# First batch of an FFT filter and softplus MLP on one core: stage A in pairs, stage B from SBUF, later weight conversions

## The chip, the cores and the metric

The kernel runs on one core of a Trainium2 chip. The metric is the device time of one execution in microseconds (us); lower is better. Before the change three runs took 2556.89, 2555.26 and 2554.69 us, with a median of 2555.26 us.

The core has five engines that run side by side, each through its own queue in order: PE (matrix products; its weight loads are listed as PEld), DVE (the vector engine), ACT (the scalar engine), POOL (GpSimd) and SP, which here only issues DMAs. ACT and POOL issue DMAs too. All DMAs run on 16 DMA engines.

## The reference

```python
X = np.fft.rfft(x, axis=1)                      # x: 8 x 3072 x 256
Y = X * (filt_r + 1j * filt_i)[None, :, :]
y = np.fft.irfft(Y, n=3072, axis=1).reshape(8 * 3072, 256)
h = y @ w_in                                    # 256 x 2048
g = np.maximum(h, 0.0) + np.log1p(np.exp(-np.abs(h)))
out = (g @ w_out).astype(np.float32)            # 2048 x 256
```

[...]

## The kernel before

**Arithmetic.** Every float32 product is three passes over operands split as hi + lo (`split_mm`, L64). A split is a rounding copy (hi) and a subtraction (lo): `hi_lo`, L75.

**Transform of one batch.** Stage A: sums and differences of the sequence's halves (`a_sum`), split, and multiplied by a 128-point matrix `ca`, for 12 values of n2 (`a_mm`, results `psa`). Between A and B the data has to change partition and free axes. Stage B: 13 groups u of 120 rows (the last has 96), split (`inh`, `inl`), multiplied by `cb`, then by the filter `fr`, `fi` on DVE (three operations t, L181 to L185, and one sum on POOL, L186). The product is split again (`zh`, `zl`) and multiplied by `cc` in stage C (`psc`, copied to `co`). After a second change of axes, stage D (`di`, `psd`, `sd`, `y`) gives 512 tokens of MLP input (`yT`) for each of 6 blocks.

**Change of axes.** In batches 1 to 7 both go through DRAM (`s1`, `s2`). In batch 0, A's results stay in SBUF (`first_s1`, 128 partitions); `b_load` (L144) copies group u by two DMAs (one for each half h) from 10 neighbouring partitions of `first_s1` to 120 partitions of a tile `bi`, and loads `fr` (256 KB) and `fi` (128 KB) of that group. These four DMAs for each u are issued by SP; `bi` and the filter's tile `ft` have three buffers each. `co` goes to DRAM (`s2`) by a DMA on ACT's queue and comes back by `d_load`.

**MLP.** 48 blocks of 512 tokens, 8 steps each: `mm1` (12 products into `h`), three ACT operations, `soft` (three DVE operations of 128x1024: `s` L294, `gh` L296, `gl` L298), and two steps later `mm2` (12 products into `o`). Pieces of the next batch's transform stand between them in fixed slots. I call the DVE operation L294 of step i "s(i)", counted from the MLP's first step.

**Weights.** Sixteen blocks k of 512 columns (0 to 7 for w_in, 8 to 15 for w_out) are loaded as raw 64-bit words and converted: six DVE operations (`weight`, L344 to L357), one ACT copy and two POOL operations (`weight_ends`, L371 to L373). `LOADS`, `CONVERSIONS` and `WEIGHTS` say when: block 0 after A's tenth piece, 1 and 2 at A's end, 3 after the first piece of B, 8, 9 and 4 after C, 5 and 11 between D and the MLP, then one block in each of the steps 0 to 6 (10, 6, 7, 12, 13, 14, 15). Within a step the conversion's operations stand between and behind the three of `soft`.

**Order.** Everything is emitted in one hand-made order (`manual_schedule`): for batch 0 by `first`, which walks through the list `seq` of pieces and loads and prepares ahead; afterwards by `Run` with its slots. Tile pools add the waits for buffers. Buffers of raw weights are shared with other tiles (`TAGS`).

Of the kernel before, what the change touches and what calls it, by code (L numbers as in the profile page):

```python
# [12 lines left out]
bits, and hi hi + hi lo + lo hi is summed in float32.  # L13
"""
# [27 lines left out]
TAGS = {1: "in", 2: "ca", 4: "in", 5: "in", 8: "in", 11: "ca"}  # whose buffers they use, if not the output's  # L42
# Twice the upper word of the least normal float32, as float64.
# [4 lines left out]
def fft_mlp(ctx: ExitStack, tc: tile.TileContext, x, fr, fi, ca, cb, cc, cd, w_in, w_out, out):  # L48
# [14 lines left out]

    def split_mm(ps, lhs, rhs, first=True, last=True):  # L64
# [18 lines left out]
    class Batch:  # L83
# [5 lines left out]
        def engines(self, first):  # L89
            """Where hi and lo of loaded data are worked out: nothing else waits for them in the first transform."""  # L90
            return (nc.vector, nc.gpsimd) if self.b or first else (nc.scalar, nc.vector)

        def a_load(self, i):
            if i == 0 and self.b:
                self.s1 = dram.tile([2, P, N2, D], F32, tag="s1", name="s1")
            if self.b or i < 6:
                xt = work.tile([P, 2, 512], F32, tag="in", name="x", bufs=3)
            else:
                xt = start.tile([P, 2, 512], F32, name=f"x{i}")
# [18 lines left out]
        def a_prep(self, i):  # L118
            if self.b or i == 0:
                self.a_sum(i)  # L120
            st = self.t.pop(("as", i))
            if self.b == 0 and i + 1 < N2:
                self.a_sum(i + 1)
            self.t["ap", i] = hi_lo(st, P, "in", *self.engines(0))

        def a_mm(self, i):
# [7 lines left out]
            if self.b == 0:  # L134
# [494 lines left out]
```

## Time and profile before

| | us |
|---|---|
| median of three runs | 2555.26 |
| span of the profiled execution, first to last instruction | 2552.2 |
| start of the first A piece on PE | 8.17 |
| start of the first B piece on PE | 36.68 |
| s(0), the first softplus operation on DVE | 137.71 |
| s(7) | 198.34 |

The profile gives no time of its own beside its span; the median of the runs is 3.1 us above the span, for what lies around it. Times in the tables of the profile are counted from the span's start. In answers that list instructions, the columns are start, duration, engine, line of the kernel, operation, output and inputs, and, in brackets, how long the engine had been idle and what released it. In the view of busy time by stages, the columns are the stage, its length, busy time and number of instructions on PE, PEld, DVE, ACT and POOL, the granted PE clock (1 is full), the mean busy share of the 16 DMA engines, and GB/s.

### The profile page before, as it was taken

How to read it: one execution, taken by the hardware profiler on the slowest of the kernel's cores; microseconds unless marked ns; L12 is line 12 of the kernel's file. 1: busy time of each engine (PE TensorE's matmuls, PEld its weight loads, DVE VectorE, ACT ScalarE, POOL GpSimd, SP SyncE). 2: the span in 40 equal slices, each digit the busy share in tenths (PEclk: the TensorE clock that was granted, in tenths of full speed). 3: DMA queues.
4: the chain of work that ended last, by engine and by line, in shares of the span. 5: the costliest groups of instructions: out<-in, count | busy, mean ns of one | idle time of the engine just before them, and what ended most of it. 6: DMA issues, size and time to landing. Idle time of an engine off the chain costs nothing.

```text
span 2552.2 us, 31099 instructions
## 1 busy us (share of the span) xinstructions
PE 2459.7 (96%) x11232; PEld 2026.3 (79%) x11232; DVE 2050.1 (80%) x2575; ACT 1494.7 (59%) x1742; POOL 747.3 (29%) x610
## 2 busy tenths in 40 slices
PE   4579999999999999999999999999999999999999
PEld 3258778888888888888888888888888888888887
DVE  7799896888878897789878888688887898766665
ACT  3355556656656665666566566566665666665555
POOL 4444341333213332233313333143221433111110
PEclk7589999999999999999999999999999999999999
DMA  7724432433224431343223432243422533111100
GB/s 209 200 83 142 124 106 73 133 117 98 71 85 143 119 98 52 104 147 107 80 76 121 130 85 82 90 128 97 117 70 70 170 103 91 44 42 34 42 17 17
DMA packets 144244, 249.97 MB, mean 98 GB/s; under 512 B 12772, under 2 KB 62052, under 8 KB 144092
## 3 DMA queue, kind: packets, MB, share of 16 engines
q1 hardware_dynamic: 91740, 149.98, 19.5%
q0 software_dynamic: 14112, 50.83, 6.9%
q10 hardware_dynamic: 38240, 47.20, 5.9%
q8 instruction: 88, 1.44, 0.2%
q14 instruction: 64, 0.52, 0.1%
HBM read 172.46 MB, written 72.35 MB: 96 GB/s over the span
## 4 chain that ended last, share of the span: by engine, by line
PE 88%; DVE 6%; DMA 2%; issue 2%; ACT 1%; SPq 0%; POOL 0%; ACTq 0%; DVEq 0%; POOLq 0%
PE h L67 39%; PE o L67 39%; PE psd L241 3%; PE psa L67 2%; PE psb L67 2%; PE psc L67 2%; DMA bi<-s 1%; DVE s L294 1%; DMA x<-in_x 1%; DVE gh L296 0%; DVE gl L298 0%; DVE raw L349 0%; DVE inh L73 0%; DVE raw L353 0%; DVE p L345 0%
## 5 line engine op out<-in xcount | busy, mean ns | idle before, releaser
L67 PE MATMUL h<-yT,wi 128*128 128x512 f32 x4608 | 1120.6, 392 | 12.7 <-DVE s L294 11.2
L67 PEld LDWEIGHTS h<-yT,wi 128*128 128x128 f32 x4608 | 859.7, 189 | 192.2 <-DVE s L294 10.2
L67 PE MATMUL o<-gh,wo 128*128 128x512 f32 x3072 | 953.1, 391 | 5.5 <-ACT ob L321 4.7
L285 ACT ACTIVATE s<-h 128x1024 f32<-128x1024 f32 x384 | 394.8, 1028 | 722.5 <-PE h L67 684.4
L67 PEld LDWEIGHTS o<-gh,wo 128*128 128x128 f32 x3072 | 568.8, 189 | 121.2 <-ACT ob L321 5.1
L294 DVE SCALAR_TENSOR_TENSOR s<-h,s 128x1024 f32<-128x1024 f32 x384 | 468.0, 1219 | 180.2 <-ACT s L287 177.9
L67 PE MATMUL o<-gl,wo 128*128 128x512 f32 x1536 | 600.3, 391 | 2.8 <-DVE gl L298 2.8
L298 DVE TENSOR_TENSOR gl<-s,gh 128x1024 fp32r<-128x1024 f32 x384 | 471.5, 1228 | 36.5 <-DVE gh L296 1.8
L286 ACT ACTIVATE s<-s 128x1024 f32<-128x1024 f32 x384 | 407.8, 1062 | 12.2
L287 ACT ACTIVATE s<-s 128x1024 f32<-128x1024 f32 x384 | 407.6, 1062 | 12.2
L296 DVE CAST gh<-s 128x1024 fp32r<-128x1024 f32 x384 | 313.2, 816 | 36.5 <-DVE s L294 2.3
L67 PEld LDWEIGHTS o<-gl,wo 128*128 128x128 f32 x1536 | 288.9, 188 | 65.8 <-DVE gl L298 4.1
L267 POOL TENSOR_TENSOR yT<-y,yT 128x512 fp32r<-128x512 f32 x94 | 126.2, 1343 | 607.1 <-DVE yT L73 607.1
L186 POOL TENSOR_TENSOR t<-t,t 128x512 f32<-128x512 f32 x104 | 147.7, 1420 | 405.7 <-DVE t L185 404.2
L79 POOL TENSOR_TENSOR inl<-bi,inh 120x512 fp32r<-120x512 f32 (+1 forms) x100 | 132.6, 1326 | 289.0 <-issue 114.3
L79 POOL TENSOR_TENSOR dil<-di,dih 128x512 fp32r<-128x512 f32 x94 | 121.4, 1291 | 208.5 <-DVE dih L73 140.4
L253 DVE TENSOR_TENSOR sd<-psd,ev 128x256 f32<-128x256 f32 x192 | 80.6, 420 | 114.9 <-ACT ev L252 114.7
L79 POOL TENSOR_TENSOR inl<-st,inh 128x512 fp32r<-128x512 f32 x84 | 118.1, 1406 | 166.8 <-DVE inh L73 165.6
L79 DVE TENSOR_TENSOR zl<-t,zh 128x512 fp32r<-128x512 f32 x104 | 90.5, 870 | 56.6 <-ACT zh L71 54.4
L241 PE MATMUL psd<-cd,dih 128*128 128x256 f32 x384 | 100.9, 285 | 11.5 <-ACT dih L71 9.8
L241 PE MATMUL psd<-cd,dil 128*128 128x256 f32 x384 | 101.8, 286 | 3.0 <-DVE dil L79 3.0
L67 PE MATMUL psb<-inh,cb_sb 120*128 120x512 f32 (+1 forms) x224 | 74.1, 416 | 20.1 <-ACT inh L71 19.1
(60 smaller groups left out, 1808.1 us busy)
## 6 DMA issues: line engine op xcount, KB each, us to landing
ft<-in_fr SPq DMA_DIRECT2D x104, 256.0 KB
x<-in_x SPq DMA_DIRECT2D x48, 512.0 KB
ca<-in_ca POOLq DMA_DIRECT2D x48, 512.0 KB, 4.7
cd<-in_cd POOLq DMA_DIRECT2D x48, 512.0 KB, 4.1
di<-s SPq DMA_DIRECT2D x96, 256.0 KB
out<-ob SPq DMA_DIRECT2D x48, 512.0 KB
s<-co ACTq DMA_DIRECT2D x96, 240.0 KB
s<-ao ACTq DMA_DIRECT2D x84, 256.0 KB
```

The costliest lines, as they stand in the source:

```text
L67: nc.tensor.matmul(out=ps, lhsT=lhs[a], rhs=rhs[b], start=first and k == 0, stop=last and k == 2)
L79: lo_eng.tensor_sub(out=lo[:p], in0=src, in1=hi[:p].bitcast(F32))
L186: nc.gpsimd.tensor_add(out=t1, in0=t1, in1=t2)
L241: nc.tensor.matmul(out=ps[:, h].rearrange("p k n -> p (k n)"), lhsT=ds[k][:, h, 128 * c:128 * c + 128], rhs=cdt[:, h, j].rearrange("p k n ...
L253: nc.vector.tensor_add(out=s[:, j], in0=ps[:, :, 0], in1=ev)
L267: lo_eng.tensor_sub(out=lo[:, c], in0=y, in1=hi[:, c].bitcast(F32))
L285: nc.scalar.activation(out=a, in_=h, func=AF.Abs)
L286: nc.scalar.activation(out=a, in_=a, func=AF.Exp, scale=-1.0)
L287: nc.scalar.activation(out=a, in_=a, func=AF.Ln, bias=1.0)
L294: nc.vector.scalar_tensor_tensor(out=a, in0=h, scalar=0.0, in1=a, op0=ALU.max, op1=ALU.add)
L296: nc.vector.tensor_copy(out=hi, in_=a)
L298: nc.vector.tensor_sub(out=lo, in0=a, in1=hi.bitcast(F32))
```

## The change

It concerns the first batch and the order of the weights; the only edit to later batches is that `b_load` now issues two DMAs instead of one.

- **Stage A by pairs** (`first_a`): two values of n2 are handled as one, with 1024 columns for hi, lo, the PSUM tile and its copy `ao`. There are again 12 sums and differences of 512 columns. x has three buffers instead of six tiles; the loads of the pairs 3, 4 and 5 are issued as buffers come free, and those of 4 and 5 behind the copies of the pairs 0 and 1 on SP.
- **A straight to B's tile**: `ao` goes by four DMAs for each pair (two of 120 rows, two of 8) into `s1_b`, an SBUF tile that has stage B's layout for all 13 groups. The constant matrix's columns are put in another order, so that a DMA of 120 rows writes 10 partitions that lie 12 apart. `bi` and its 26 DMAs are gone.
- **Filter ahead** (`filter_load`): each of the 13 groups has its own tile. Groups 0 to 5 are loaded between the copies of the last three pairs, 6 to 12 behind the raw blocks 0, 1, 2.
- **lo in B**: on DVE for u = 0, 1, 2, 3, 5, 7, 9, 11 (before 0, 2, 3, 7), otherwise on POOL.
- **First block's inverse on chip** (`c_mm`): beside the DMA to DRAM, two small DMAs on SP bring each `co` of batch 0 into block 0's tile `di`.
- **Weights**: no block is converted in A. Block 0 is converted ahead of B's first preparation, 1 at B's end, 2 and 8 between C and D, and the other twelve in the steps 0 to 7: (3, 9), (4), (5, 10), (6, 11), (7, 12), (13), (14), (15).
- The late pools lie on the other side of SBUF and wait tile by tile.

```diff
-LOADS = {("a", 8): (0,), ("a", 10): (2, 3), ("c", 9): (9,), ("c", 11): (8, 4), ("d", 1): (11,), ("y", 0): (5,)}
-CONVERSIONS = {("a", 9): (0,), ("a", 11): (1, 2), ("b", 0): (3,), ("c", 12): (8, 9, 4)}
-WEIGHTS = (5, 11), (10,), (6,), (7,), (12,), (13,), (14,), (15,)
+WEIGHTS = (3, 9), (4,), (5, 10), (6, 11), (7, 12), (13,), (14,), (15,)
...
         def b_load(self, u):
-            if self.b == 0:
-                for h in range(2):
-                    nc.sync.dma_start(
-                        out=bt[:p, 256 * h:256 * h + 256],
-                        in_=first_s1[h][10 * u:10 * u + p // N2],
-                    )
...
+            for h in range(2):
+                nc.sync.dma_start(out=bt[:p, 256 * h:256 * h + 256], in_=rows[:, :, h])
...
-            self.t["bp", u] = hi_lo(self.t["b", u][0][:p], p, "in", hi_eng, lo_eng if u in (0, 2, 3, 7) else nc.gpsimd)
+            self.t["bp", u] = hi_lo(src[:p], p, "in", hi_eng, lo_eng if u < 3 or u % 2 else nc.gpsimd)
...
+            if self.b == 0:
+                dt = self.t["d", 0][0]
+                for n in range(2):
+                    nc.sync.dma_start(
+                        out=dt[10 * u:10 * u + p // N2, :, n],
+                        in_=co[:p].rearrange("(r n) (h d) -> n r h d", n=N2, h=2)[n],
+                    )
...
+    def first_a(s1_b, first_pool):
...
+            for p in range(NP):
+                if p + 3 < NP:
+                    load_x(p + 3)
+                if p + 1 < NP:
+                    sums(p + 1)
...
+                nc.vector.tensor_sub(out=lo, in0=st, in1=hi.bitcast(F32))
+                ps = ps_h.tile([P, 2, 512], F32, tag="h", name="psa")
...
+                ao = work.tile([P, 2, 512], F32, tag="ob", name="ao")
+                nc.scalar.activation(out=ao, in_=ps, func=AF.Copy)
+                for j in range(2):
+                    d = slice(256 * j, 256 * j + 256)
+                    for rows, q, u in ((120, slice(0, 120), slice(0, 12)), (96, slice(120, 128), 12)):
+                        nc.sync.dma_start(
+                            out=s1_b[:rows].rearrange("(r n) u c -> n r u c", n=N2)[2 * p + j][:, u],
+                            in_=ao[q, :, d],
+                        )
+                if p >= 3:
+                    filters.update(filter_load(p - 3, first_pool))
...
+    def first_bc(s1_b, filters, pool):
+        bt.a_done()
+        for k in (0, 1, 2):
+            weight_load(k)
+        for u in range(NU):
+            if u not in filters:
+                filters.update(filter_load(u // 2, pool))
...
+        for k in (8, 3):
+            weight_load(k)
+        together((0,))
+        weight_ends()
+        bt.b_prep(0)
+        for i in range(NU + 2):
+            if i + 1 < NU:
+                bt.b_prep(i + 1)
+            if i < NU:
+                bt.b_mm(i)
+            if 0 < i <= NU:
+                bt.z_mm(i - 1)
+            if i == NU - 1:
+                together((1,))
+                weight_ends()
+            if i >= 2:
+                bt.c_mm(i - 2)
...
+    def first_d():
+        together((2, 8))
+        weight_ends()
+        bt.d_prep(0)
+        bt.d_prep(1)
...
-                soft(s, chain(*(weight(k) for k in (WEIGHTS[s + 1] if s + 1 < len(WEIGHTS) else ()))))
+                soft(s, chain(*(weight(k) for k in (WEIGHTS[s] if s < len(WEIGHTS) else ()))))
```

On SP, the queue of the DMAs, stage A's end and the first two groups of B looked like this before (`s_82` and `s_83` are the two halves of `first_s1`, `raw` a block of weights):

```order
L100 DMA x_109<-in_x 128x2x512
L330 DMA raw<-in_w_in 128x1024 x3
L149 DMA bi<-s_82 120x1x256
L149 DMA bi<-s_83 120x1x256
L159 DMA ft<-in_fr 128x512
L160 DMA ft<-in_fi 64x512
```

The same place on SP after the change, between stage A's last pair and the first raw blocks (the rows L523 are the copies of the last pair, `fr` and `fi` the filter):

```order
L465 DMA fr_258<-in_fr 128x512
L466 DMA fi_254<-in_fi 64x512
L523 DMA s1b<-ao 10x24x256
L523 DMA s1b<-ao 8x2x256
L523 DMA s1b<-ao 10x24x256
L523 DMA s1b<-ao 8x2x256
L465 DMA fr_283<-in_fr 128x512
L466 DMA fi_282<-in_fi 64x512
L465 DMA fr_286<-in_fr 128x512
L466 DMA fi_282<-in_fi 64x512
L326 DMA raw<-in_w_in 128x1024 x3
```

The copies that B waits for have moved from B's loop to the end of A, behind part of the filter, and the raw blocks from ahead of them to behind them.

On DVE, the first step of the MLP and the start of the second stood like this before (a block of weights is m, p, raw, raw, p, raw):

```order
L294 SCALAR_TENSOR_TENSOR s<-h,s 128x1024
L344 TENSOR_SCALAR m<-raw 128x512
L345 TENSOR_SCALAR p<-raw 128x512
L296 CAST gh<-s 128x1024
L349 SCALAR_TENSOR_TENSOR raw<-raw,p 128x512
L298 TENSOR_TENSOR gl<-s,gh 128x1024
L353 SCALAR_TENSOR_TENSOR raw<-m,raw 128x512
L355 TENSOR_SCALAR p<-raw 128x512
L357 SCALAR_TENSOR_TENSOR raw<-raw,p 128x512
L73 CAST dih<-di 128x512
```

The same step on DVE after the change:

```order
L290 SCALAR_TENSOR_TENSOR s<-h,s 128x1024
L340 TENSOR_SCALAR m<-raw 128x512
L341 TENSOR_SCALAR p<-raw 128x512
L292 CAST gh<-s 128x1024
L345 SCALAR_TENSOR_TENSOR raw<-raw,p 128x512
L294 TENSOR_TENSOR gl<-s,gh 128x1024
L349 SCALAR_TENSOR_TENSOR raw<-m,raw 128x512
L351 TENSOR_SCALAR p<-raw 128x512
L353 SCALAR_TENSOR_TENSOR raw<-raw,p 128x512
L340 TENSOR_SCALAR m<-raw 128x512
L341 TENSOR_SCALAR p<-raw 128x512
L345 SCALAR_TENSOR_TENSOR raw<-raw,p 128x512
```

A second block's six operations now stand behind those of the first, ahead of the next step's s.

More of the change, by code (lines that the diff above doesn't have):

```diff
@@ L93, in a_load @@
         def a_load(self, i):
-            if i == 0 and self.b:
+            if i == 0:
                 self.s1 = dram.tile([2, P, N2, D], F32, tag="s1", name="s1")
[L96 to L99, printed above, removed]
+            xt = work.tile([P, 2, 512], F32, tag="in", name="x", bufs=3)
             nc.sync.dma_start(
@@ L459, in fft_mlp, with filter_load @@
             slots[free[at + len(va) + GAP + k * (56 - at - len(va) - GAP) // len(vb)]].append(p)
+    def filter_load(v, pool):
+        fit = pool.tile([P, 512], F32, name=f"fi{v}")
+        found = {}
+        for u in range(2 * v, min(2 * v + 2, NU)):
+            frt = pool.tile([P, 512], F32, name=f"fr{u}")
+            half = fit[64 * (u % 2):64 * (u % 2) + 64]
+            nc.sync.dma_start(out=frt, in_=fr[u])
+            nc.sync.dma_start(out=half, in_=fi[u])
+            found[u] = frt, half
+        return found
@@ new lines, in first_bc @@
+    def first_bc(s1_b, filters, pool):
[5 more added lines that the diff above has]
+                filters.update(filter_load(u // 2, pool))
+            bt.t["b", u] = s1_b[:, u], *filters[u]
+            if u == 8:
+                bt.e_load(0)
+                bt.t["d", 0] = work.tile([P, 2, 2, D], F32, tag="di", name="di"), bt.t.pop(("e", 0))
+        for k in (8, 3):
[15 more added lines that the diff above has]
+                bt.c_mm(i - 2)
+        for k in (9, 4):
+            weight_load(k)
+        bt.done += "c" * NU
@@ L461, in fft_mlp @@
+    def first_d():
[3 more added lines that the diff above has]
+        bt.d_prep(1)
+        for n, (_, k, i) in enumerate(d_visits(0)):
+            getattr(bt, f"{k}_mm")(i)
     with tc.manual_schedule():
         nc.scalar.preload_act_table_set("natural_log_exp_and_others")
-        def first(part):
-            for q in part:
-                p = seq[q][1:]
-                run.ahead(q)
-                if p == ("c", 2):
-                    batches[0].e_load(0)
-                run.do(q)
-                for k in LOADS.get(p, ()):
-                    weight_load(k)
-                together(CONVERSIONS.get(p, ()))
-                weight_ends()
@@ L475, in fft_mlp @@
-        seq = visits(batches[0], "a") + visits(batches[0], "b") + d_visits(0)
-        run = Run([[p] for p in seq], 2)
-        b_end = seq.index((batches[0], "b", NU - 1)) + 1
-        with tc.tile_pool(name="first", bufs=1) as first_pool:
-            first_s1 = [first_pool.tile([P, N2, D], F32, name=f"s1{h}") for h in range(2)]
-            with tc.tile_pool(name="start", bufs=1) as start:
-                for i in range(NP):
-                    if i == NP - 1:
-                        weight_load(1)
-                    batches[0].a_load(2 * i)
-                nc.gpsimd.dma_start(out=cb_sb, in_=cb)
-                nc.gpsimd.dma_start(out=cc_sb, in_=cc)
-                run.classes[0]["load"] = NP
-                first(range(N2))
-            first(range(N2, b_end))
@@ L491, in fft_mlp @@
-        late = ctx.enter_context(tc.tile_pool(name="late", bufs=1))
-        wo = [late.tile([P, 16, D], F32R, name=f"wo{k}") for k in range(2)]
-        mlp = ctx.enter_context(tc.tile_pool(name="mlp", bufs=2))
-        first(range(b_end, len(seq)))
-        together(WEIGHTS[0])
-        for k in WEIGHTS[1]:
-            weight_load(k)
+        bt = batches[0]
+        with tc.tile_pool(name="first", bufs=1, **other) as first_pool:
+            s1_b = first_pool.tile([P, NU, 512], F32, name="s1b")
+            filters = first_a(s1_b, first_pool)
+            with tc.tile_pool(name="filter", bufs=1, **other) as pool:
+                first_bc(s1_b, filters, pool)
@@ L540, in _constants @@
             inv[h, n2] = fwd[h, n2].T * (2 / S)
+    order = [10 * u + r for r in range(10) for u in range(NU - 1)] + list(range(120, 128))
+    fwd = fwd[..., order]
     pairs = lambda a: np.stack(parts(a), 3).reshape(2, NP, 2, 128, 2, 128).transpose(1, 3, 0, 2, 4, 5)
```

74 lines of the change are left out of this document (54 added, 20 removed).

## The prediction

> **What bounds the kernel now.** First the page: its line of busy times, two rows of the 40 slices and the shares of the chain that ended last.
>
> ```profile
> PE 2459.7 (96%) x11232; PEld 2026.3 (79%) x11232; DVE 2050.1 (80%) x2575; ACT 1494.7 (59%) x1742; POOL 747.3 (29%) x610
> ...
> PE   4579999999999999999999999999999999999999
> ...
> DVE  7799896888878897789878888688887898766665
> ...
> PE 88%; DVE 6%; DMA 2%; issue 2%; ACT 1%; SPq 0%; POOL 0%; ACTq 0%; DVEq 0%; POOLq 0%
> ```
>
> PE is full from the fourth slice on, and 88% of the chain is PE's; what the change touches lies in the first three slices (64 us each). So next the busy times by stage: A; B and C; up to the first MLP product; the steps in which weights are still converted; the rest.
>
> ```profile
> core 0: us, PE busy (x) PEld busy (x) DVE busy (x) ACT busy (x) POOL busy (x), PEclk, DMA share, GB/s
> 0.00:36.70 36.70, 16.24 (x73) 12.98 (x73) 26.53 (x43) 17.57 (x29) 9.04 (x15) 0.83 0.77 260
> 36.70:108.90 72.20, 43.50 (x83) 21.05 (x83) 53.32 (x63) 22.13 (x38) 38.11 (x29) 0.52 0.69 174
> 108.90:130.70 21.80, 7.51 (x22) 4.74 (x20) 19.11 (x31) 6.16 (x12) 10.97 (x7) 0.50 0.56 182
> 130.70:203.70 73.00, 58.70 (x226) 45.43 (x227) 71.75 (x96) 34.68 (x41) 33.61 (x27) 0.89 0.25 80
> 203.70:2552.20 2348.50, 2333.78 (x10833) 1942.07 (x10831) 1879.37 (x2347) 1414.18 (x1623) 655.54 (x533) 1.00 0.31 93
> ```
>
> In the last stage PE has 14.7 us of idle time in 2348.5: its length is PE's work, which the change leaves as it is. In the fourth stage DVE has 1.3 us of idle time in 73: DVE sets it. So the question is only when DVE is through with everything ahead of the ninth step, and DVE's idle time is the reserve: 10.2 us in A, 18.9 in B and C, 2.7 and 1.3 behind them, 33 in all. The change has to cut this, for DVE's work stays (12 sums, 16 blocks, 13 groups; four more lo of B).
>
> **Stage A, to the first t.** The last x of A lands at 22.37, behind 7.34 MB (6 x, 6 ca, cb, cc and one raw block); the second row is the full rate of that time, 397 GB/s.
>
> ```profile
> 22.37 0.69 DVE L116 TENSOR_TENSOR st<-x 128x512 f32<-128x512 f32 x1 [1.46 <-DMA x<-in_x]
> ...
> 6.00:18.00 12.00, 9.19 (x41) 7.84 (x42) 8.90 (x14) 7.53 (x14) 0.00 (x0) 1.00 1.10 397
> ```
>
> Without the raw block (0.524 MB, 1.3 us) that is 21.1. To it come the copies into s1_b, 512 packets of 1 KB for a pair, and the filter of four groups ahead of the last pair's (1.57 MB, 4.0 us). The trace has no such copy. The two nearest are bi's, alone in 30.9 to 32.4, and co's way to DRAM in 108 to 110: packets, MB, and their share of 16 engines.
>
> ```profile
> q1 hardware_dynamic: 94, 0.09, 45.0%
> ...
> q10 hardware_dynamic: 286, 0.27, 46.0%
> ```
>
> bi: 1.5 x 16 x 0.45 / 94 = 115 ns a packet; co: 2 x 16 x 0.46 / 286 = 51 ns. bi alone kept 0.45 of the engines busy, seven at a time, so I take ten engines for a copy with ten rows on one side, 51 packets each. I take co's 52 ns, as it too reads 120 partitions: 2.7 us a pair, 16.2 for six. Bounds: 16 engines at 51 ns, 1.6 us a pair (6.6 us less in all); ten at 115 ns, 5.9 (19 us more). Sum: 21.1 + 16.2 + 4.0 = 41.3 for the last copy's landing. Compute hides beside this: sums, hi, lo and 12 products of a pair take DVE, ACT and PE under 3 us each. SP issues 12 copies and 8 filter loads behind the third pair; two bi take it 1.65 us (rows below), so 12 x 0.8 + 8 x 0.9, 17 us from about 25 on: it ends no later than the transfers.
>
> [...]
>
> Block 0's raw words stand behind those copies and two more groups on SP, and DVE's conversion of them stands ahead of B's first lo: every inl, t and zl is queued behind it. One block alone took DVE 25.02 to 28.42, 3.4 us; the first inl started 3 us before the first t (39.62).
>
> ```profile
> 25.02 0.43 DVE L344 TENSOR_SCALAR m<-raw 128x512 uint32<-128x512 uint32 x1
> ...
> 27.73 0.69 DVE L357 SCALAR_TENSOR_TENSOR raw<-raw,p 128x512 f32<-128x512 uint32 x1
> ...
> 36.66 1.64 DVE L79 TENSOR_TENSOR inl<-bi,inh 120x512 fp32r<-120x512 f32 x1
> ```
>
> 41.3 + 2.2 (raw words, 1.3 of it transfer) + 3.4 + 3.0 = **50** for the first t, 10.4 later than now. DVE's idle time in A grows from 10 to about 30 us: 12 sums and 6 lo of double width are all that it has.
>
> **B and C.** The first row has 13 t, from 39.6 to 102.3: 62.7 us. SP's queue shows the pace: a new pair of bi every 4.8 us.
>
> ```profile
> L181 DVE TENSOR_TENSOR t<-psb,ft x13: 677/692/693, 39.6 to 102.3; 128x512 f32<-128x512 f32 x13
> ...
> 49.29 1.64 SPq L149 DMA_DIRECT2D bi<-s  x2
> ...
> 54.09 1.65 SPq L149 DMA_DIRECT2D bi<-s  x2
> ...
> 48.80 0.68 DVE L181 TENSOR_TENSOR t<-psb,ft 128x512 f32<-128x512 f32 x1
> ...
> 50.91 0.69 DVE L79 TENSOR_TENSOR zl<-t,zh 128x512 fp32r<-128x512 f32 x1
> 51.52 1.76 DVE L79 TENSOR_TENSOR inl<-bi,inh 120x512 fp32r<-120x512 f32 x1
> 53.21 0.68 DVE L181 TENSOR_TENSOR t<-psb,ft 128x512 f32<-128x512 f32 x1
> ...
> 58.56 0.69 DVE L181 TENSOR_TENSOR t<-psb,ft 128x512 f32<-128x512 f32 x1
> ...
> 61.47 0.69 DVE L181 TENSOR_TENSOR t<-psb,ft 128x512 f32<-128x512 f32 x1
> ```
>
> With bi and filter in place DVE is late next. A round without lo takes 2.9 us (58.56 to 61.47), one with lo on DVE 4.4 (48.80 to 53.21; the lo takes 1.76, as POOL's sum of t runs beside it). The new order has one round of 3.8 (no zl), five of 4.4, six of 2.9: 43 us, 19.7 less. By the second row of the stages PE was busy 43.5 us for these 13 rounds, at a clock of 0.52, ACT 22.1 and POOL 38.1, all no more than DVE's new 43, though PE and POOL are close behind. Bounds: all rounds 2.9, 35; as now, 62.7. So the last t starts at 93, 9 us earlier.
>
> **C to the first softplus.** Now 102.3 to 121.20, 18.9 us, three blocks among it. Then: the last t's and zl 2.7, block 1 3.4, zl 0.6, blocks 2 and 8 together 5.6 (108.87 to 114.50), 2 for POOL beside them (the two dil below take 3.22 where two operations of 0.6 would do): 14.3. Block 0's di comes by small copies beside this. So dil starts at 107.6, **13.6 earlier**; from there to s(0), 16.5 us, nothing changes.
>
> ```profile
> 108.87 0.42 DVE L344 TENSOR_SCALAR m<-raw 128x512 uint32<-128x512 uint32 x1
> ...
> 114.50 0.42 DVE L344 TENSOR_SCALAR m<-raw 128x512 uint32<-128x512 uint32 x1
> ...
> 121.20 3.22 DVE L79 TENSOR_TENSOR dil<-di,dih 128x512 fp32r<-128x512 f32 x2
> ...
> 137.71 1.23 DVE L294 SCALAR_TENSOR_TENSOR s<-h,s 128x1024 f32<-128x1024 f32 x1 [0.36 <-ACT s L287]
> ```
>
> **The steps with weights.** Here seven blocks were converted; 5 and 11 filled DVE's wait for s(0), 131.3 to 136.9, which now stays empty. Then there are twelve.
>
> ```profile
> 148.98 1.21 DVE L294 SCALAR_TENSOR_TENSOR s<-h,s 128x1024 f32<-128x1024 f32 x1
> ...
> 173.11 1.22 DVE L294 SCALAR_TENSOR_TENSOR s<-h,s 128x1024 f32<-128x1024 f32 x1
> ...
> 179.05 1.22 DVE L294 SCALAR_TENSOR_TENSOR s<-h,s 128x1024 f32<-128x1024 f32 x1
> ...
> 180.51 1.27 DVE L345 TENSOR_SCALAR p<-raw 128x512 uint32<-128x512 uint32 x1
> ```
>
> A step with one block takes 5.94 us (173.11 to 179.05). Five more blocks at 3.4: 17.0. POOL's operations brake DVE: for one block 0.9 (the p at 180.51 takes 1.27, not 0.42), for the pair (5, 11) 4.9 (137.71 to 148.98 is 11.27; less 5.94 and 0.4 for dih). Before: one pair and six or seven singles, about 11 us; then four pairs and four singles, 4 x 1.8 + 3.6 = 10.8 to 4 x 4.9 + 3.6 = 23.2. I take the middle, 6 more. The raw block 7 can be loaded only when POOL is through with 6 in the very step whose s is followed by 7's conversion: ACT 0.65, POOL 1.6 + 1.1, load some 3, less DVE's own 1.1: up to 5 us of waiting, of which the brake would have taken a part; I add 2. Together **25 later**, bounds 20 and 34.
>
> **Sum.** -13.6 + 25 = +11.4: span 2552.2 + 11.4 = 2563.6, and with the 3.1 us around it **2567**. The idle time tells the same: 20 us more in A and 6 ahead of s(0), against 19 less in B and C. The 91 more bi issues of later batches cost nothing: SP issues them slots ahead, beside a PE that is 99% busy.
>
> **Rivals.**
> - *Late blocks weigh little* (same): no more braking than 2.7, no wait for block 7, and copies on 16 engines: -13.6 - 6.6 + 19.7 = -0.5, 2555. For it: single blocks brake by 0.9 only. Against: the one pair that the trace shows braked 4.9.
> - *PE takes over* (faster): from the first MLP product on PE, not DVE, sets the steps, and late conversions go into DVE's slack; the 13.6 are kept: 2542. It decides if DVE has 17 us free in the fourth stage; it has 1.3. For it only that PE is busy 58.7 of 73.
> - *Slow copies* (much slower): s1_b's packets cost bi's 115 ns, +19: 2586. About the same if the change does not free B: rounds set by the chain from t over POOL and ACT to zl, not by the transfers, then 62.7 us stay and it is +20.
>
> **How the numbers follow.** Forecast 0.47 (2560 to 2573), late blocks light 0.20, slow 0.17, PE takes over 0.16. A measurement can tell 0.2%, 5 us, from no change: slower 0.64, same 0.20, faster 0.16. The range 2547 to 2588 leaves out the PE case and a little beyond the slow one; it covers loops at 2.9 us and the bounds of copies and late blocks.
>
> **What would show it.** The first t near 50 and the last copy's landing near 41; thirteen t in some 43 us with rounds of 2.9 and 4.4; dil near 108; s(0) near 124 with DVE idle 6 us ahead of it; s(7) near 208 instead of 198.34; a wait for raw in s(4)'s step. Wrong if the first t comes before 42 or after 60, or if PE never waits for s after s(2).

## The result, and the profile after

| | before | after |
|---|---|---|
| median of the runs, us | 2556.07 (4 runs, 2554.69 to 2557.27) | 2602.47 (4 runs, 2599.04 to 2604.55) |
| ratio, 95% interval | | 1.0179 (1.0166 to 1.0191) |
| span of the profiled execution, us | 2552.2 | 2597.3 |

The changed kernel is 1.8% slower, 46 us; the forecast was 2567, and its range ended at 2588. The profiled spans differ by 45.1 us, and the runs by about as much, so the traces can be compared line by line.

First the page of the changed kernel: busy times, two rows of slices, the shares of the chain.

```profile
PE 2483.1 (96%) x11232; PEld 2029.1 (78%) x11232; DVE 2046.6 (79%) x2573; ACT 1495.1 (58%) x1730; POOL 742.5 (29%) x606
...
PE   3668999999999999999999999999999999999999
...
DVE  4898897788868888789877888688886888766665
...
PE 87%; DVE 7%; issue 1%; ACT 1%; POOL 0%; DMA 0%; SPq 0%; DVEq 0%; ACTq 0%; POOLq 0%
```

DVE's work is 3.5 us less (2050.1 before). But PE has 23.4 us more busy time (2459.7 before) for the same 11232 products, at a granted clock of 1.00 in both from 220 to 2500 us. That is half of the loss.

Where it arises is told by the transfers of the finished blocks, one per 512 tokens. The rows are the groups of that tile, before and after; the last figures are the starts of the first and of the 48th.

```profile
L323 SPq DMA_DIRECT2D out<-ob x48: 372/389/398, 209.9 to 2548.1; - x48
```
```profile
L319 SPq DMA_DIRECT2D out<-ob x48: 373/389/514, 230.1 to 2593.3; - x48
```

The first one is 20.2 us late, the last 45.2. Single rows say how the distance grows: the second block is 23.3 us late (261.39 and 284.68), the 41st 40.7 (below). So there are two losses: **23 us before the second block, and 22 us, about half a microsecond a block, nearly evenly over the other 46.**

```profile
2235.85 0.39 SPq L323 DMA_DIRECT2D out<-ob  x1
```
```profile
2276.59 0.39 SPq L319 DMA_DIRECT2D out<-ob  x1
```

**The even loss.** The page's costliest group is the first MLP product. Before, then after:

```profile
L67 PE MATMUL h<-yT,wi 128*128 128x512 f32 x4608 | 1120.6, 392 | 12.7 <-DVE s L294 11.2
...
L67 PE MATMUL o<-gh,wo 128*128 128x512 f32 x3072 | 953.1, 391 | 5.5 <-ACT ob L321 4.7
...
L67 PE MATMUL o<-gl,wo 128*128 128x512 f32 x1536 | 600.3, 391 | 2.8 <-DVE gl L298 2.8
```
```profile
L67 PE MATMUL h<-yT,wi 128*128 128x512 f32 x4608 | 1145.8, 397 | 18.5 <-ACT wi L367 8.0
...
L67 PE MATMUL o<-gh,wo 128*128 128x512 f32 x3072 | 958.5, 393 | 23.4 <-POOL wo L369 13.7
...
L67 PE MATMUL o<-gl,wo 128*128 128x512 f32 x1536 | 603.3, 393 | 0.6 <-DVE gl L294 0.6
```

h takes 5 ns more a product, 25.2 us over 4608; the products of o take 8.4 us more (5.4 with gh, 3.0 with gl). Products overlap in time (before, one h lasts 392 ns in the mean, and the next starts 227 ns behind it, in the median), so these sums are more than the 23.4 us of PE's busy time. In the timeline of PE one step's twelve h are one row; late in the run, where nothing else is on PE between them, before and after:

```profile
2456.46 2.88 PE L67 MATMUL h<-yT,wi 128*128 128x512 f32 x12
```
```profile
2459.74 2.96 PE L67 MATMUL h<-yT,wi 128*128 128x512 f32 x12
```

The same twelve instructions, the same clock, no wait, and yet 0.08 us more. Nothing in the diff touches `mm1`. What the change does touch is where yT lies in SBUF, the on-chip memory: the late pools moved to its other side.

**The loss at the start.** The stages of the changed kernel, cut at the first lo of B, the end of the t, s(0) and s(8):

```profile
0.00:55.90 55.90, 15.40 (x72) 14.07 (x72) 17.88 (x24) 14.71 (x16) 5.53 (x14) 0.76 0.88 268
55.90:103.60 47.70, 35.68 (x80) 21.18 (x80) 44.37 (x58) 19.81 (x35) 29.25 (x19) 0.54 0.47 128
103.60:133.30 29.70, 16.20 (x46) 10.86 (x44) 19.20 (x33) 10.90 (x18) 13.91 (x9) 0.58 0.30 98
133.30:219.20 85.90, 54.94 (x192) 39.98 (x191) 84.50 (x112) 34.08 (x40) 38.08 (x30) 0.82 0.28 92
```

DVE's idle time up to s(8) is 38.0 + 3.3 + 10.5 + 1.4 = 53.3 us of 219.2; before, it was 33 of 203.7. DVE's work there fell by 4.8, so s(8) comes 15.5 us later. B and C are as quick as forecast; the idle time is in stage A. DVE's rows there:

```profile
23.55 0.69 DVE L490 TENSOR_TENSOR st<-x 128x512 f32<-128x512 f32 x1 [7.00 <-DMA x<-in_x]
...
29.90 0.69 DVE L490 TENSOR_TENSOR st<-x 128x512 f32<-128x512 f32 x1 [3.92 <-DMA x<-in_x]
...
52.48 0.43 DVE L340 TENSOR_SCALAR m<-raw 128x512 uint32<-128x512 uint32 x1 [18.88 <-DMA raw<-in_w_in]
...
58.96 0.68 DVE L169 TENSOR_TENSOR t<-psb,fr 128x512 f32<-128x512 f32 x1
```

DVE is through with A's last lo at 33.6 and then waits 18.9 us for the raw words of block 0. SP's queue in that time (a row's length covers the waits between its transfers):

```profile
12.17 3.38 SPq L523 DMA_DIRECT2D s1b<-ao  x4
...
16.36 3.47 SPq L523 DMA_DIRECT2D s1b<-ao  x4
...
20.41 12.39 SPq L523 DMA_DIRECT2D s1b<-ao  x8
...
35.72 3.25 SPq L523 DMA_DIRECT2D s1b<-ao  x4
...
41.33 3.25 SPq L523 DMA_DIRECT2D s1b<-ao  x4
...
46.97 1.47 SPq L326 DMA_DIRECT2D raw<-in_w_in  x3
```

The last copy is issued near 44, and its last packet ends at 46.6; the raw block is issued at 47, behind four filter loads. Later PE waits for weights rather than for s. Two of these waits, near the end of the steps:

```profile
213.55 0.80 PE L67 MATMUL o<-gh,wo 128*128 128x512 f32 x1 [5.42 <-POOL wo L369]
224.51 0.79 PE L67 MATMUL o<-gh,wo 128*128 128x512 f32 x1 [2.78 <-POOL wo L369]
```

### The profile page after: what moved, and what is told of

It reads as the page before. It is cut to its first block, busy times and chain, and to the rows that moved or that the text cites. A ratio compares the mean times of both kernels' runs of the same rounds, so it can differ in the third digit from the quotient of the medians.

```text
span 2597.3 us, 31294 instructions
## 1 busy us (share of the span) xinstructions
PE 2483.1 (96%) x11232; PEld 2029.1 (78%) x11232; DVE 2046.6 (79%) x2573; ACT 1495.1 (58%) x1730; POOL 742.5 (29%) x606
## 3 DMA queue, kind: packets, MB, share of 16 engines
q1 hardware_dynamic: 92712, 149.98, 18.3%
## 4 chain that ended last, share of the span: by engine, by line
PE 87%; DVE 7%; issue 1%; ACT 1%; POOL 0%; DMA 0%; SPq 0%; DVEq 0%; ACTq 0%; POOLq 0%
PE h L67 39%; PE o L67 38%; PE psd L237 3%; PE psa L67 2%; PE psb L67 2%; PE psc L67 2%; DVE s L290 1%; DVE gh L292 1%; DVE gl L294 0%; DVE p L341 0%; DVE m L340 0%; DVE t L173 0%; DVE inh L73 0%; DVE t L169 0%; DVE t L170 0%
## 5 line engine op out<-in xcount | busy, mean ns | idle before, releaser
L67 PE MATMUL h<-yT,wi 128*128 128x512 f32 x4608 | 1145.8, 397 | 18.5 <-ACT wi L367 8.0
L67 PE MATMUL o<-gh,wo 128*128 128x512 f32 x3072 | 958.5, 393 | 23.4 <-POOL wo L369 13.7
L282 ACT ACTIVATE s<-s 128x1024 f32<-128x1024 f32 x384 | 407.9, 1062 | 12.2
L283 ACT ACTIVATE s<-s 128x1024 f32<-128x1024 f32 x384 | 407.4, 1061 | 12.2
L79 POOL TENSOR_TENSOR inl<-bi,inh 120x512 fp32r<-120x512 f32 (+1 forms) x91 | 120.5, 1324 | 277.3 <-DVE inh L73 207.7
L79 DVE TENSOR_TENSOR zl<-t,zh 128x512 fp32r<-128x512 f32 x104 | 83.2, 800 | 47.9 <-ACT zh L71 45.3
L237 PE MATMUL psd<-cd,dil 128*128 128x256 f32 x384 | 100.6, 283 | 0.7 <-DVE dil L79 0.7
L71 ACT ACTIVATE zh<-t 128x512 fp32r<-128x512 f32 x104 | 65.1, 626 | 60.3 <-POOL t L174 56.6
```

The source lines that it names most:

```text
L79: lo_eng.tensor_sub(out=lo[:p], in0=src, in1=hi[:p].bitcast(F32))
L237: nc.tensor.matmul(out=ps[:, h].rearrange("p k n -> p (k n)"), lhsT=ds[k][:, h, 128 * c:128 * c + 128], rhs=cdt[:, h, j].rearrange("p k n ...
L282: nc.scalar.activation(out=a, in_=a, func=AF.Exp, scale=-1.0)
L283: nc.scalar.activation(out=a, in_=a, func=AF.Ln, bias=1.0)
```

## The experiments

Milestones of the traces, in us: start of the first and the 13th t, of the first dil on DVE, of s(0) and s(8), of the first block's transfer; then the median of the runs beside the kernel before in the same series.

| kernel | t 1 | t 13 | dil | s(0) | s(8) | out 1 | median | ratio (95%) |
|---|---|---|---|---|---|---|---|---|
| before | 39.6 | 102.3 | 121.2 | 137.7 | 203.7 | 209.9 | 2555 to 2556 | |
| changed | 59.0 | 101.5 | 116.9 | 133.3 | 219.3 | 230.1 | 2602.5 | 1.0179 (1.0166 to 1.0191) |
| x_ahead | 58.2 | 100.6 | 115.9 | 132.4 | 218.2 | 229.0 | 2601.1 | 1.0181 (1.0164 to 1.0198) |
| raw_ahead | 51.8 | 99.4 | 114.8 | 131.2 | 217.3 | 228.4 | 2598.3 | 1.0167 (1.0151 to 1.0182) |
| filter_pool | 64.3 | 106.8 | 122.2 | 138.4 | 224.4 | 235.4 | 2606.1 | 1.0198 (1.0182 to 1.0213) |
| block3 | 61.0 | 103.5 | 118.9 | 135.3 | 217.5 | 229.2 | 2598.9 | 1.0165 (1.0151 to 1.0179) |
| all_undone | 55.2 | 100.0 | 109.9 | 125.8 | 197.4 | 207.9 | 2553.9 | 0.9990 (0.9981 to 0.9999) |
| earlier | 56.0 | 100.5 | 110.3 | 125.8 | 200.0 | 206.1 | 2551.7 | 0.9987 (0.9978 to 0.9996) |

Kernels that leave stage A untouched (changed, block3 and those with an inserted tile in the next section) have their first t between 59.0 and 61.3, so a microsecond or two there is chance. Runs of the changed kernel itself lie up to 5.5 us apart (2599.0 to 2604.6), so a gain of 4 us in a median is at the edge of what can be told.

### Four places for yT: the 32-byte tiles

The pools on the right side grow downward from the end of a partition, and in this program their tiles begin 32 bytes below a multiple of 256; on the left, everything in the MLP began on a multiple of 512. The addresses here and below come from the program's layout and the sizes of the inserted tiles; the profile lists none. My first theory was that a multiple of 64 counts.

```diff
+        pad = ctx.enter_context(tc.tile_pool(name="pad", bufs=1, **other))
+        pad.tile([P, 8], F32, name="pad")
         with tc.tile_pool(name="first", bufs=1, **other) as first_pool:
```

> The changed kernel with one tile of 32 bytes at the upper end of the partition, so that the tiles of the pools on the right side (start, first, filter, late, mlp) begin at multiples of 64 bytes instead of 32 behind one. Nothing else changes. Theory 1 (addresses): yT's place makes each product of yT and wi 5 ns longer (232 ns from start to start against 227 before), and that is the drift of some 22 us over the later blocks: the mean of MATMUL h goes from 397 back to 392 ns, the out transfers keep a constant distance of 20 to 23 us to those of before, and the time falls from 2602 to about 2580. Rival 1 (later batches: bi in two transfers, other row order) and rival 2 (the right side itself, that is the distance from wi): 2602, MATMUL h stays at 397 ns.

Measured: 2603.1, ratio 1.0188 (1.0173 to 1.0203). Nothing was repaired; MATMUL h stayed at 397 ns. The theory fell in this form, but the same series had the counter-test, the kernel before with 32 bytes inserted:

```diff
         wo = [late.tile([P, 16, D], F32R, name=f"wo{k}") for k in range(2)]
+        late.tile([P, 8], F32, name="pad")
```

> The kernel before with one tile of 32 bytes between wo and the pool with yT, s, gh and gl; these then begin 32 bytes behind a multiple of 64, wi and wo stay. Theory 1 in the form that yT alone counts: MATMUL h 397 instead of 392 ns, o unchanged, 2556 + 23 = 2579. In the form that any moving operand off the multiple of 64 counts whose stationary operand is on it (h and o alike): h and o both 5 ns longer, 2556 + 46 = 2602. Rivals 1 and 2: 2556.

Measured: **2599.5, ratio 1.0172 (1.0157 to 1.0187): 32 unused bytes cost the old kernel 44 us.** Rivals 1 and 2 are out: no piece of the change is in this kernel. Its page shows h slowed as in the changed kernel, and o with it (24.8, 13.4 and 6.2 us more than before, 44.4 together):

```profile
L67 PE MATMUL h<-yT,wi 128*128 128x512 f32 x4608 | 1145.4, 397 | 13.0 <-DVE s L294 11.6
...
L67 PE MATMUL o<-gh,wo 128*128 128x512 f32 x3072 | 966.5, 395 | 4.8 <-ACT ob L321 4.8
...
L67 PE MATMUL o<-gl,wo 128*128 128x512 f32 x1536 | 606.5, 395 | 2.3 <-DVE gl L298 2.3
```

The third kernel has the tile of 32 bytes in the changed kernel between wo and the pool with yT and gh:

```diff
         wo = [late.tile([P, 16, D], F32R, name=f"wo{k}") for k in range(2)]
+        pad = ctx.enter_context(tc.tile_pool(name="pad", bufs=1, **other))
+        pad.tile([P, 8], F32, name="pad")
         mlp = ctx.enter_context(tc.tile_pool(name="mlp", bufs=2, **other))
```

> The changed kernel with the tile of 32 bytes between wo and the pool with yT, s, gh and gl: these on multiples of 64, wo still 32 behind one. Theory 1, yT alone counts: as with the tile ahead of both, about 2580. In the form that the two operands of a product must stand alike: h is repaired and o becomes 5 ns longer, 2580 + 23 = 2602. Rivals 1 and 2: 2602.

Measured: 2619.0, ratio 1.0250 (1.0235 to 1.0266). h was not repaired, and o, which the changed kernel still ran at the old pace, became slow as well. So it isn't one operand's place: o is fast where gh and wo are shifted alike and slow where only one is.

### The period: 480, 224 and 352 bytes

The same edit as the first with another size (`[P, 120]`, `[P, 56]`, `[P, 88]`).

> The changed kernel with a tile of 480 bytes at the upper end of the partition: yT, s, gh, gl and wo begin at multiples of 512. The four runs with 32 bytes showed that a multiple of 64 is not what counts (232 ns a product of h there too) and that products were slow wherever the moving and the stationary tile's addresses differ in their last 9 bits (h and o of the kernel before with the tile, h and o of the changed kernel with it behind wo, h of the changed kernel) and fast where they are the same (o of the changed kernel, h and o before). Theory 1b: what counts is that yT and wi have the same address modulo 512, wi's blocks being 512 bytes apart: here they have, so h goes from start to start in 227 ns, the mean of MATMUL h is 392, and the time falls by the drift, 22 us, to 2580. Rival (the right side itself slows h, whatever the address): 2602.

> The same with a tile of 224 bytes: the tiles on the right begin 256 bytes behind a multiple of 512, wi on a multiple. Theory 1b with a period of 512: h stays slow (232 ns), o is fast (gh and wo alike), 2602. With a period of 256 or less: h is fast, 2580. PE's products of B and C with cb and cc, which lie 128 bytes off, take 232 to 236 ns in both kernels and speak for more than 128.

> The changed kernel with a tile of 352 bytes: the tiles on the right begin 128 bytes behind a multiple of 256, wi on a multiple. The tiles of 480 and 224 bytes (0 and 256 off) both gave 227 ns a product of h, the tile of 32 bytes (192 off) 233. If the period of theory 1b is 256, h is slow here (232 ns from start to start) and the time near 2600; if it is 128, h is fast and the time near 2577. For 256 speak the products with cb, 128 off, which took 232 ns in every kernel.

Measured: 2577.0 (ratio 1.0081, 1.0066 to 1.0096), 2577.4 (1.0086, 1.0069 to 1.0103) and 2602.0 (1.0184, 1.0168 to 1.0200). One step's h in the three kernels:

```profile
2457.14 2.88 PE L67 MATMUL h<-yT,wi 128*128 128x512 f32 x12
```
```profile
2455.52 2.88 PE L67 MATMUL h<-yT,wi 128*128 128x512 f32 x12
```
```profile
2455.41 2.96 PE L67 MATMUL h<-yT,wi 128*128 128x512 f32 x12
```

All eight kernels together, with addresses modulo 256 and the median distance of the starts of two products that follow each other:

| kernel | yT, wi | h, ns | gh, wo | o, ns | time, us |
|---|---|---|---|---|---|
| before | 0, 0 | 227 | 0, 0 | 227 | 2556 |
| changed | 224, 0 | 232 | 224, 224 | 227 | 2602.5 |
| pad_all | 192, 0 | 233 | 192, 192 | 229 | 2603.1 |
| before_pad | 32, 0 | 234 | 32, 0 | 234 | 2599.5 |
| pad_mlp | 192, 0 | 233 | 192, 224 | 232 | 2619.0 |
| pad_480 | 0, 0 | 227 | 0, 0 | 227 | 2577.0 |
| pad_224 | 0, 0 | 227 | 0, 0 | 227 | 2577.4 |
| pad_352 | 128, 0 | 232 | 128, 128 | 227 | 2602.0 |

In all sixteen cases the product is fast (227 to 229 ns) where the moving tile (yT, gh) and the stationary tile (wi, wo) have the same address modulo 256, and slow (232 to 234) where they don't. The period is neither 512 (256 apart is fast: h of pad_224, 227 ns) nor 128 (128 apart is slow: h of pad_352, 232). The right side as such costs nothing (h and o of pad_480, 227). With 480 bytes the drift is gone: the second finished block leaves 24.0 us later than in the kernel before, the last one 22.9. So this is 25 us of the 46.

### Stage A: x ahead, raw words ahead, the filter on POOL

```diff
-            xts[p] = work.tile([P, 2, 512], F32, tag="in", name="x", bufs=3)
+            tag = "di" if p in (3, 4) else "in"
+            xts[p] = work.tile([P, 2, 512], F32, tag=tag, name="x", bufs=2 if tag == "di" else 3)
...
             load_ca(3)
+            load_x(3)
+            load_x(4)
             sums(0)
+            load_x(5)
             for p in range(NP):
-                if p + 3 < NP:
-                    load_x(p + 3)
```

> The changed kernel with the loads of pairs 3, 4 and 5 of x on SP ahead of all copies into s1_b (pairs 3 and 4 in di's buffers, which are free there). Theory 2: the late landing of the last copy (last packet 46.6, forecast 41.3) comes from x 4 and x 5, which stand behind copies on SP, with lo of pairs 3 and 4 behind the sums that wait for them: DVE's waits of 7.0 and 3.9 us for x shrink to below 3 in all, the last packet lands near 41.5, the first t starts near 54 instead of 59, and the time falls by 5 to 2597. Rival: the copies' 24 issues and the filter's on SP, or their transfers, set the landing anyway: last packet within 1.5 us of 46.6, time 2602.

Measured: 2601.1, within chance of the changed kernel's 2602.5. DVE's waits for x went as they should, and nothing came of it:

```profile
12.13 20.45 SPq L525 DMA_DIRECT2D s1b<-ao  x16
```
```profile
23.86 1.02 ACT L521 ACTIVATE ao<-psa 128x1024 f32<-128x1024 f32 x1 [7.23 <-DMA s1b<-ao]
...
28.40 1.02 ACT L521 ACTIVATE ao<-psa 128x1024 f32<-128x1024 f32 x1 [2.58 <-DMA s1b<-ao]
...
36.09 1.02 ACT L521 ACTIVATE ao<-psa 128x1024 f32<-128x1024 f32 x1 [4.26 <-DMA s1b<-ao]
```

ACT's ao now waits instead, for the copies out of its two buffers to finish, and the next pair's hi is queued behind it; SP worked on the first four pairs' copies until 32.6 as before. Theory 2 fell: x was not the cause, it only stood where the copies' own wait stands otherwise.

```diff
-TAGS = {0: "in", 1: "in", 2: "in", 3: "ca", 8: "ca", 10: "in", 12: "in"}
+TAGS = {0: "di", 1: "in", 2: "in", 3: "ca", 8: "ca", 10: "in", 12: "in"}
...
+            weight_load(0)
             sums(0)
...
-        for k in (0, 1, 2):
+        for k in (1, 2):
```

> The changed kernel with the raw words of block 0 loaded into a di buffer ahead of the copies (on SP, behind the first three x), its conversion where it stands in DVE's order. Theory 2b: DVE's wait of 18.9 us before B ends with the raw words at 52.5, not with the last copy (46.6 + landing); without it DVE converts block 0 in the wait and the first t starts near 51 instead of 59, s(0) 8 earlier, the time 8 less: 2594. Rival: s1_b's landing and the filter's set the first t, 57 or later, or the gain is lost again in the steps with weights, because PE then waits for them: 2600 to 2603.

Measured: 2598.3, about 4 us less. The first t came 7.1 us earlier, as theory 2b said, but the thirteenth only 2.1. The first row below is the wait that is left ahead of B (its inh, which waits for the copies, ends just before it, whatever releaser the row names); the wait in the second row, inside B, is new:

```profile
49.83 1.29 DVE L79 TENSOR_TENSOR inl<-s1b,inh 120x512 fp32r<-120x512 f32 x2 [12.78 <-DMA fr<-in_fr]
...
75.72 1.35 DVE L79 TENSOR_TENSOR zl<-t,zh 128x512 fp32r<-128x512 f32 x1 [4.41 <-ACT zh L71]
```
```profile
ACT co L193 <- DMA di<-co: 7.0, 1, 7.0
```
```profile
66.48 0.36 SPq L326 DMA_DIRECT2D raw<-in_w_in  x1
67.38 32.67 SPq L202 DMA_DIRECT2D di<-co  x20
```

ACT's third co waits 7.0 us for a buffer whose small copies into block 0's di are issued at 67.4 only, behind the filter loads and raw blocks on SP; zh, and with it DVE's zl, is queued behind it. A wait removed in front of a loop brought out the next one in the same queue. This trace also gives the landing of the copies apart from the raw words: ACT's first inh, released by the copies, starts at 49.17, and the copies' last packet ends at 48.24, 0.9 us before.

```diff
-    def filter_load(v, pool):
+    def filter_load(v, pool, eng=nc.sync):
...
-            nc.sync.dma_start(out=frt, in_=fr[u])
-            nc.sync.dma_start(out=half, in_=fi[u])
+            eng.dma_start(out=frt, in_=fr[u])
+            eng.dma_start(out=half, in_=fi[u])
...
-                    filters.update(filter_load(p - 3, first_pool))
+                    filters.update(filter_load(p - 3, first_pool, nc.gpsimd))
```

> The changed kernel with the filter's twelve loads of stage A issued by POOL instead of SP. Loading x ahead removed both waits for x and moved the last packet of the copies by 0.3 us only: SP was busy without a gap from 29.7 to 48.4, with 0.81 us for a copy and 0.54 for a filter load. Theory 2c (SP's issues set the landing): without eight filter loads ahead of the last copy, 4.4 us, the last packet is at 42 to 43 instead of 46.6, the raw words of block 0 come 5 to 6 earlier (their issue moves by all twelve, 6.6), the first t starts at 53 to 54 and the time is 5 to 6 less, 2597. Rival: the transfers' own time sets the landing: within 1.5 us of 46.6, time 2602.

Measured: 2606.1, slower than the changed kernel. The edit does more than it was meant to: on POOL the filter loads wait for no copy and start at 16 instead of 33, in front of x's last load.

```profile
40.62 0.69 DVE L490 TENSOR_TENSOR st<-x 128x512 f32<-128x512 f32 x1 [11.88 <-DMA x<-in_x]
```

x's last load was issued at 19.95, as in the changed kernel (19.93), but the sum that needs it starts at 40.62 instead of 29.90: beside the filter's transfers it took longer. As a test of SP's issue the run is inconclusive.

### The steps: block 3

```diff
-WEIGHTS = (3, 9), (4,), (5, 10), (6, 11), (7, 12), (13,), (14,), (15,)
+WEIGHTS = (9,), (4,), (5, 10), (6, 11), (7, 12), (13,), (14,), (15,)
...
         for n, (_, k, i) in enumerate(d_visits(0)):
             getattr(bt, f"{k}_mm")(i)
+        together((3,))
```

> The changed kernel with block 3's conversion taken out of the first step and put behind the transform's last piece, into DVE's wait of 6.5 us for the first softplus; the first step then has block 9 alone. Theory 3 (DVE sets the steps with weights, and a late block costs its 3.4 us and the brake of a pair): s(1) comes 4 to 6 us earlier, s(8) and the first out with it, the time falls by 4 to 6 to 2597. Rival: PE's waits for the weights' lo from POOL (13.7 us on wo in the changed kernel) set the steps, and what DVE gains is lost in them: s(8) less than 2 us earlier, 2601 to 2603.

Measured: 2598.9, 3.6 us less. From s(0) to s(8) it took 217.46 - 135.31 = 82.15 us instead of 85.93 (85.8 to 86.1 in all the kernels that have the same steps): **a late block costs 3.8 us**, and the end of the MLP's first steps follows DVE. Of the gain at s(8) one microsecond was gone by the first transfer, in PE's waits.

```profile
135.31 1.23 DVE L290 SCALAR_TENSOR_TENSOR s<-h,s 128x1024 f32<-128x1024 f32 x1 [3.16 <-ACT s L283]
...
217.46 1.22 DVE L290 SCALAR_TENSOR_TENSOR s<-h,s 128x1024 f32<-128x1024 f32 x1
```

### All of it together

```diff
-WEIGHTS = (3, 9), (4,), (5, 10), (6, 11), (7, 12), (13,), (14,), (15,)
+WEIGHTS = (10,), (5,), (6,), (11, 7), (12,), (13,), (14,), (15,)
...
             load_ca(3)
+            load_x(3)
+            load_x(4)
             sums(0)
+            load_x(5)
+            weight_load(0)
+            weight_load(1)
...
+                if p in (3, 4):
+                    together((p - 3,))
+                    weight_ends()
...
+                if p == 3:
+                    for k in (2, 3):
+                        weight_load(k)
+                    filters.update(filter_load(0, first_pool))
+                if p == 4:
+                    weight_load(4)
+            for v in (1, 2):
+                filters.update(filter_load(v, first_pool))
+            for k in (2, 3, 4):
+                together((k,))
+                weight_ends()
...
+            if i % 2 == 0:
+                load(i // 2 + 3)
...
-        together((2, 8))
+        together((8,))
...
+        together((9,))
...
+        pad.tile([P, 120], F32, name="pad")
```

> The changed kernel with what the runs so far blame taken away together: the tile of 480 bytes (-22, the drift); x ahead of the copies, raw words 0 to 4 loaded among the copies, blocks 0 to 4 converted in DVE's waits of stage A instead of behind B, before the first D piece and in the first two steps; the filter of groups 2 to 5 behind the last copy and that of 6 to 12 between the first small copies of co; block 9 in the wait for s(0); eight blocks left in the steps. Theories 1b, 2b and 3 together: first t 49 to 53, thirteen t in 42 to 44 us, dil near 99 (116.85), s(0) near 115 (133.3), s(8) 66 to 70 us later near 183 (before: 203.7), the later blocks at the pace of before: 2556 - 20 = 2536, between 2530 and 2545, faster than both kernels. Rival: stage A is bound by its transfers and the five raw blocks move the first t back to 58 or later, or PE's waits for weights take up the gain: 2550 or more.

Measured: 2553.9, ratio 0.9990 (0.9981 to 0.9999) against the kernel before, 49 us less than the changed kernel. Less than expected: the first t came at 55.2, s(8) 6.3 us earlier than before instead of 20, and PE's waits for wo took 4 of these again. (Nine blocks stay in the steps; the expectation miscounts them as eight.) Busy times from 0 to s(8), then PE's waits from 100 to 330:

```profile
0.00:197.40 197.40, 119.48 (x382) 85.31 (x383) 164.62 (x227) 78.62 (x107) 85.25 (x71) 0.74 0.52 162
```
```profile
PE o L67 <- POOL wo L369: 11.7, 4, 5.4
PE h L67 <- DVE s L290: 6.0, 5, 1.8
```

DVE is idle for 32.8 us there, as much as before the change (33), and what is saved is DVE's work alone, 6.1 us. The five blocks do fill waits of A, but with their raw words among the copies the last copy's packet ends at 50.9 instead of 46.6, and B cannot start before that.

```diff
-WEIGHTS = (10,), (5,), (6,), (11, 7), (12,), (13,), (14,), (15,)
+WEIGHTS = (10, 5), (6,), (11, 7), (12,), (13,), (14,), (15,)
...
-                if p == 3:
-                    for k in (2, 3):
-                        weight_load(k)
-                    filters.update(filter_load(0, first_pool))
-                if p == 4:
-                    weight_load(4)
+                for k in {2: (2, 3), 3: (4,)}.get(p, ()):
+                    weight_load(k)
+                if p == 4:
+                    filters.update(filter_load(0, first_pool))
...
         together((9,))
+        weight_load(6)
```

> The last kernel with two moves. In stage A the raw words of blocks 2, 3 and 4 are loaded one pair of copies earlier and the first filter loads one pair later: there DVE waited 5.1 and 2.3 us for raw words (to 37.7 and 48.7), so the first t should start near 51 instead of 55 and s(0) 4 earlier. And the blocks of the steps are converted one step earlier (10 and 5 in the first, 6, then 11 and 7, 12, 13, 14, 15), because PE waited 11.7 us there for wo from POOL: the first out should come 4 (first move) to 10 us (both) earlier, 2550 to 2544. Rival: the copies' landing, not the raw words, set the first t, and DVE's work sets the steps wherever blocks stand in them: 2552 to 2554.

Measured: 2551.7, ratio 0.9987 (0.9978 to 0.9996), the lowest median of all, though its interval overlaps that of the kernel above. The first move missed: the first t stayed at 56, since now the copies landed later (their last packet ends at 52.1, and ACT's first inh waits for them until 53.31). The second did what it says, no wait for wo is left, but PE waits for s in its place:

```profile
PE h L67 <- DVE s L290: 20.5, 6, 7.1
```
```profile
0.00:200.00 200.00, 121.02 (x392) 86.94 (x393) 165.16 (x228) 78.59 (x107) 87.49 (x73) 0.72 0.51 160
```

DVE's idle time up to s(8) (200.0) is 34.8 us here. The rival of this run was right on both counts.

## Why the prediction was wrong, point by point

**The step that failed first: "its length is PE's work, which the change leaves as it is".** I counted PE's products and saw that none was added. The change gave them other addresses, and h's 4608 products take 5 ns more each. With the address repaired and everything else as changed, the time is 2577.0: 10 us above the forecast and inside its range. The list of changes had the sentence on the other side of SBUF; no term, bound or rival answered to it. The trace of before held one hint: products of B and C with cb and cc, whose address is 128 bytes off, start 233 to 234 ns apart there, those of h 227 (medians behind 600 us). I had not compared them. A sentence "the operands of 9216 products move" would have put the doubt where it belonged.

**The landing of the copies: 41.3 forecast, about 47.5 measured.** The last packet ends at 46.6; the 0.9 us behind it is taken from raw_ahead, so 47.5 is an estimate. The price of a packet was right: in 28 to 31 one of the changed kernel's packets took 3 x 16 x 0.645 / 594 = 52 ns, where I had taken 52. Some of them are x's; in 31 to 33, with the copies alone, it is 2 x 16 x 0.55 / 345 = 51 ns. The ten engines of the sum were my choice: the trace of before had bi at seven, and no run shows how many a copy is given. The busy share (64.5% and 55.0% of sixteen) is that of ten engines in the first stretch and of nine in the second, near that choice.

```profile
q1 hardware_dynamic: 594, 0.64, 64.5%
```

That these packets would cost co's 52 ns and not bi's 115 was a choice between two measured values. It held; why bi's cost more is not shown, for no run changed one difference between the two kinds of copy alone.

Wrong was the sum, which laid the transfers end to end and had SP ending "no later than the transfers" at 42. SP needs 3.25 us for the four copies of a pair, where the transfers were to take 2.7, and 2.2 for four filter loads. From the fourth pair on it issues without a gap, from 29.7 to 44.6, while the DMA engines are busy for 0.75 of the time: there, as far as this trace tells, SP's issues set the pace and not the transfers. I had them start at about 25. Why the fourth pair starts only at 29.7 is **not settled**. The pairs' copies start at 12.2, 16.4, 20.4 and 29.7; x ahead showed one thing that the sum lacked, that a third pair's ao cannot be written before the first pair's copies are finished, so that transfers, ACT, and SP's issues follow each other in a ring. With x ahead the last packet stayed where it was (46.3), with the filter on POOL it came at 55.3, and with more raw words in front at 50.9 and 52.1. (The sum's 7.34 MB are 7.31 by the sizes of the tiles, which changes it by 0.1 us.)

**Block 0's raw words: 2.2 us forecast behind the landing, about 5 measured** (47.5 to 52.5). They are issued at 47.0, behind the four filter loads, and take 5.5 us from there. That the conversion stands ahead of every inl was right, and raw_ahead shows its weight: 7.1 us on the first t. Together the first t came at 59.0 instead of 50.

**B and C: right.** 13 t in 42.5 us, forecast 43, bounds 35 and 62.7, in rounds of 2.7 to 2.9 and 4.4; from there to dil 15.4, forecast 14.3. So dil came 4.4 us earlier than before instead of 13.6, 9.0 of the 9.2 us that are missing inherited from A, and s(0) at 133.3 instead of 124, with the forecast idle time ahead of it (6.5 us).

**The late blocks: near in size, wrong in what PE waits for.** I had them 25 us later at the ninth step. From s(0) to s(8) the changed kernel lost 19.9 us (85.93 against 66.01), which is the 17.0 of five blocks' work and 2.9 more; for the brake and block 7 I had 8. s(7) came at 211.1, forecast 208. To the first block's transfer the loss is 24.6 us and to the second block's 27.7: that these lie near 25 is partly luck, since what comes behind s(8) fits PE's waits for wo (5.4 and 2.8 us, the rows above), which the sum did not have. block3 gives 3.8 us a block, where I had 3.4 and a brake. The sign I had named, PE waiting for s after s(2), did not come at all. PE's one wait for s is ahead of it:

```profile
134.60 0.95 PE L67 MATMUL h<-yT,wi 128*128 128x512 f32 x3 [0.91 <-DVE s L290]
```

s(2) starts at 153.2, and from s(0) to the second transfer PE waits 32.9 us for converted weights: 18.3 for wo, 14.6 for wi. By the sign that I had set, the steps' mechanism was wrong there. What stays right is that DVE's work sets their length: it was busy for 84.5 of 85.9 us, and one block fewer saved 3.8. But PE meets that work through the weights, which go from DVE over ACT and POOL, and not through s. A wait for raw in s(4)'s step did not come.

**The rivals.** "Late blocks weigh little" had the steps right to s(8) (19.7 forecast, 19.9 measured) and the copies wrong, which it had landing early. "PE takes over" was out by DVE's 1.4 us of idle time in the steps. "Slow copies" was the nearest in time (2586) and wrong in its mechanism: the packets were quick (52 ns, not 115).

The sum of the steps by what was measured: -4.4 for s(0), +27.7 for the late blocks up to the second transfer (with about 1 us of slower h in it), +21.9 for the slower h behind it: 45.2 us.

## What to carry to other kernels

When a change moves tiles to another pool or side, compare the addresses of the two operands of the costliest product: in these kernels it took 227 to 229 ns from start to start where they were equal modulo 256, and 232 to 234 where they weren't; 32 unused bytes cost 44 us here, and 480 unused bytes repaired 25. When work is moved to fill an engine's waits, sum that engine's idle time up to the point where another takes over: here the two arrangements that beat the old kernel, by 0.1%, had DVE idle for 33 to 35 us of the start, as the old one has, and gained no more than what DVE no longer had to do. And count a queue's waits for the buffers of what it carries, not only its issues and packets, before calling a chain of copies transfer-bound.

## What the runs showed of the hardware

In the traces of the eight kernels of the table, a float32r product of 512 columns (h or o) is followed by the next 227 to 229 ns later (medians) where the moving tile and the stationary tile have the same byte address modulo 256 in their partitions, and 232 to 234 ns later where they don't (offsets tried: 32, 128, 192 and 224; 32 against 0 alone cost 44 us on 9216 products). Where both are shifted alike (128, 192, 224) it is 227 to 229. The granted clock was 1.00 from 220 to 2500 us in the kernel before and the changed one; its mean over the profiled execution was 0.972 to 0.977 in all eight. In pad_all and pad_352 the pace of o also changed within a step: in the steps between 2452 and 2463 us the first six of the twelve o, which follow slow h, took 1.39 us from start to start, 232 ns each, and the five behind them 1.13 to 1.14, 226 to 228 each. What makes the pace follow the two addresses is not shown; measured is what it cost, 5 to 7 ns a product.
